# Scores and gate logits of an attention-plus-experts kernel, cut into more and smaller matmul tiles

## The chip, the cores and the metric

The kernel runs on one core of a Trainium2 chip (trn2). The metric is the device time of one execution in microseconds (us), the median of several runs; lower is better. TensorE is called PE here; a matmul on it consists of a load of the stationary operand (in the profile "PEld", LDWEIGHTS) and the streaming of the moving operand (MATMUL).

## What is computed

Chunked attention on four batches and eight heads (768 positions, head size 64), then a layer of eight experts with a fixed capacity. In numpy, cut to what matters:

```python
for c in range(S // 32):                      # chunks of 32 queries
    k_full = concat([mem_k, k[l_start:r_end]])     # 8 memory keys, 16 left, 32, 8 right
    a = softmax(q_c @ k_full.T / 8)
    out[c] = a @ v_full
x = out as (B*S, H*D) = (3072, 512)
logits = x @ w_gate                           # 8 experts
expert_idx, gate_w = argmax, its softmax probability
for e in range(8):                            # at most 80 tokens each, those of largest gate_w
    h = relu(x[tok_idx] @ w1[e]);  out[tok_idx] = gate_w * (h @ w2[e])
```

## The kernel before, in words

**Units and rounds.** Attention is cut into 32 units: a pair of heads (one on partitions 0 to 63, the other on 64 to 127), half of the sequence (384 queries in four groups of 96). Four units, the four head pairs of one batch and one half, make a round of 384 tokens; there are eight rounds.

**One unit.** Keys and queries are turned on PE (`turn_k` L325, `turn_q` L304) into `kT` and `qT`. `scores` (L773) makes, for each of the two heads, a tile `sp` of 128 keys by 384 queries. First one bf16 matmul a head adds the window mask for all queries (L779); then, for each of the four groups, one fp32 matmul a head (L786) has the group's 128 keys as stationary operand and its 96 queries as moving operand. As the heads lie on different partition halves, the two matmuls use different row halves of the array. ACT takes the exponential (L794). `values` (L351, matmul L357) multiplies with the values, 24 fp32 matmuls with 32 queries as stationary operand, into four column quarters of 32. DVE divides (L362), `turn_x` (L371) turns the output to `xT`, 128 channels by 384 tokens, which ACT copies to SBUF (L377).

**The gate of a round.** When the four `xT` of a round exist, `Ranks.steps` (L610) gives a list of small steps, two of which are popped in each later unit, between the other work. The first (`weigh`, L415) runs `gate_parts` (L384): four fp32 matmuls with a part of `w_gate` (padded from 8 to 32 columns, `wgc`) as stationary operand and 384 tokens as moving operand, one in each column quarter, which leaves four partial sums on four partition groups; ACT copies them (`lus`). The second (`logits`, L419) sums and turns them: three fp32 matmuls with 128 tokens of `lus` as stationary operand and a 0/1 matrix `sel4` as moving operand (L422). The later steps rank the tokens of each expert (L467 to L608).

**The last round** has no units behind it. Its logits are summed early (`early`, L806, matmul L810): for each of the four channel parts and three token groups one fp32 matmul with 128 tokens of `xT` as stationary operand and 8 columns of `wgc` as moving operand.

**Order.** The order of instructions on each engine is the order of the trace of the loop L852 to L905, fixed by `in_order`. The DMA queue SP loads keys and queries two head pairs ahead, values six units ahead, and in each unit two more pieces of 256 KB: expert weights or zeros for the output. After attention, 16 weight matrices of 2 MB (five of them already there) feed the experts (L1029 to L1063), at most about seven pieces in flight (`paced`, L162). The experts' matmuls (L1043, L1057) have 64 columns of weights as stationary operand and 80 tokens as moving operand.

Of the kernel before, what the change touches and what calls it, by code (L numbers as in the profile page):

```python
# [24 lines left out]
NG = 4  # L25
HT = NG * GQ
# [36 lines left out]
def kernel(  # L63
# [22 lines left out]
    NT = HT // 128  # L86
    NR = 2 * B
# [16 lines left out]
    const = ctx.enter_context(tc.tile_pool(name="const", bufs=1))  # L104
# [8 lines left out]
    mkey = masks[:, : 2 * WK].rearrange("p (f k) -> p f k", f=2)  # L113
    mqry = masks[:, 2 * WK : 2 * WK + 2 * HT].rearrange("p (f q) -> p f q", f=2)
    tok = masks[:, 2 * WK + 2 * HT :].rearrange("p (i m) -> p i m", i=2)
    wgc = const.tile([128, HP, 32], F32, name="wgc")
    sel4 = const.tile([128, E], F32, name="sel4")
    identb = const.tile([128, 128], BF16, name="identb")
    selq = const.tile([128, E], BF16, name="selq")

# [259 lines left out]
        def store(self, r, xr):  # L380
            nc.sync.dma_start(xd[r * HT : r * HT + HT, :].rearrange("(t p) d -> p t d", p=128), xr)


    def gate_parts(xTs, lu):  # L384

        for c in range(HP):
            nc.tensor.matmul(
                lu[32 * c : 32 * c + 32, :HT], lhsT=wgc[:, c, :], rhs=xTs[c], start=True, stop=True
            )

    full = [128, NT, E]

    class Ranks:
# [3 lines left out]
        def __init__(self, gt, ps_t):  # L397
            self.gt, self.ps_t = gt, ps_t
            tiles = dict(
                lus=([128, HT], F32), lmax=([128, NT], F32), lg=(full, F32), first=(full, F32),  # L400
                best=([128, NT], F32), el=(full, F32), oh=([128, NT, 4, E], BF16), gw=([128, NT], F32),
                ohg=(full, F32), rest=(full, F32), desc=([128, NT, ND, E], BF16), gbs=([128, HT], F32),
                ohT=([3 * E, HT], BF16), less=([128, NT, HT], BF16), older_=([128, NT, cap], BF16),
                beaten=([128, NT], F32), slo=([cap, E], BF16), hoto=([cap, E, cap], BF16),
                mores=([32 * NT, HT], BF16), own=(full, F32), ahead=([128, NT], F32), slot=([128, NT], BF16),
                hot=([128, NT, cap], BF16), left=([cap, E], BF16), stays=([cap, ND, E], F32),
                enters=([128, NT], F32), held=([cap, ND * E], F32), tab=([cap, ND, E], BF16), tabT=([3 * E, cap], BF16),
            )
            for name, (shape, kind) in tiles.items():
                setattr(self, name, gt.tile(shape, kind, name=name))  # L410
# [1 line left out]
        def ps(self, name, kind=F32):  # L412
            return self.ps_t.tile([128, 512 if kind == F32 else 1024], kind, name=name, tag="t")

        def weigh(self, xTs, lu):  # L415
            gate_parts(xTs, lu)
            nc.scalar.copy(self.lus, lu[:, :HT])

        def logits(self):  # L419
            lp = self.ps("lp")  # L420
            for t in range(NT):
                nc.tensor.matmul(  # L422
                    lp[:, E * t : E * t + E], lhsT=self.lus[:, 128 * t : 128 * t + 128], rhs=sel4,
                    start=True, stop=True,
                )
            self.largest(lp)

        def largest(self, lp):
# [178 lines left out]
            )  # L607
            nc.scalar.copy(self.tabT, tp[: 3 * E, :cap])  # L608

        def steps(self, r, xTs, lu):  # L610

            def fifth():
                self.turn_oh()
                self.count(0)
                self.count(1)

            def sixth():
                if r:
                    self.rivals()
                    self.beat()  # L620
                self.count(2)

            def seventh():
                if r:
                    self.older()
                self.sum_counts()

            return [
                lambda: self.weigh(xTs, lu), lambda: (self.logits(), self.gates()), lambda: None,
                lambda: (self.spread(), self.parts(r)), fifth, sixth, seventh,  # L630
                lambda: self.slots(r, self.turn_counts()), lambda: self.fill_old(r),
                lambda: self.hold(self.fill_new(r)), self.turn_table,
            ]
# [77 lines left out]
    with ExitStack() as actx:  # L711
# [16 lines left out]
        at.load_mv(0)  # L728
        at.load_v(0, 0)
        make_identity(nc, ident)  # L730
        nc.gpsimd.memset(wgc, 0.0)
        nc.scalar.dma_start(wgc[:, :, :E], moe_w_gate.rearrange("(c p) e -> p c e", p=128))

        def for_gates():
            prefi = gt.tile([128, E], I32, name="prefi")
            nc.gpsimd.iota(prefi, pattern=[[-1, E]], base=E, channel_multiplier=0)
            nc.gpsimd.tensor_copy(pref, prefi)
            by_q = ident.rearrange("p (q r e) -> p r e q", q=4, e=E)[:, 0]
            nc.vector.tensor_reduce(sel4, by_q, axis=AX, op=Alu.add)
            with nc.allow_low_precision("ones and zeros"):  # L740
                nc.vector.tensor_reduce(selq, by_q, axis=AX, op=Alu.add)
            nc.gpsimd.tensor_copy(identb, ident)
# [28 lines left out]
        P, o, xr, xTs, lus = {}, {}, {}, {}, {}  # L771

        def scores(i):  # L773
            n, f = units[i]
            sp = [ps_s.tile([WK, NG, GQ], F32, name="sp", tag="s") for e in range(2)]

            for e in range(2):
                r = slice(64 * e, 64 * e + 64)
                nc.tensor.matmul(  # L779
                    sp[e].rearrange("p g q -> p (g q)"), lhsT=mkey[r, f, :], rhs=mqry[r, f, :],  # L780
                    start=True, stop=False,
                )
            for g in range(NG):
                for e in range(2):
                    r = slice(64 * e, 64 * e + 64)
                    nc.tensor.matmul(  # L786
                        sp[e][:, g], lhsT=at.kT[n][r, NG * f + g, :],
                        rhs=at.qT[n][r, HT * f + GQ * g : HT * f + GQ * g + GQ], start=False,
                        stop=g == NG - 1,
                    )  # L790
            P[i] = []
            for e in range(2):
                P[i].append(wk.tile([WK, NG, GQ], F32, name="P", tag="P"))
                nc.scalar.activation(P[i][e], sp[e], Act.Exp, scale=scale)  # L794
# [11 lines left out]
        def early(cs, lp):  # L806

            for c in cs:
                for t in range(NT):
                    nc.tensor.matmul(  # L810
                        lp[:, E * t : E * t + E], lhsT=xTs[HP * (NR - 1) + c][:, 128 * t : 128 * t + 128],
                        rhs=wgc[:, c, :E], start=False, stop=c == HP - 1 and t == NT - 1,
                    )


        turns = {0: [("k", 2), ("q", 2)], 1: [("k", 3), ("q", 3)]}
        for n in range(HP, NP):
            i = 2 * n - 6
# [4 lines left out]
        ranks = Ranks(gt, ps_x)  # L823
        start = len(list(nc.cur_bb.bb.instructions))
# [27 lines left out]
        for i in range(NU):  # L852
            n, f = units[i]
            r = i // HP
            if i + 1 < NU:
                scores(i + 1)
# [14 lines left out]
                at.turn_q(i + 2)  # L871
            values(i)
            if i and i % HP == 0:
                lus[r] = ps_x.tile([128, 512], F32, name="lu", tag="t")
                steps = ranks.steps(r - 1, [xTs[i - HP + c] for c in range(HP)], lus[r])
# [37 lines left out]
        r = NR - 1  # L913
# [234 lines left out]
    with tc.If(redo[1] > 0):  # L1148

        with ExitStack() as actx:  # L1150
# [5 lines left out]
            ps_l = actx.enter_context(tc.tile_pool(name="ps_l2", bufs=1, space=PSUM))  # L1156
            at = Attention(actx, ps_t, wpool.tile([128, 4, F], F32, name="ld2", tag=f"w{WR0}", bufs=1))
# [5 lines left out]
            ranks = Ranks(gt, ps_t)  # L1163
            for i, (n, f) in enumerate((HP * b + c, f) for b in range(B) for f in range(2) for c in range(HP)):
                r, c = i // HP, i % HP
# [42 lines left out]
                xTs.append(at.turn_x(i, xr, ps_t.tile([128, 512], F32, name="xt2", tag="t")))  # L1208
                if c == HP - 1:
                    at.store(r, xr)  # L1210
                    steps = ranks.steps(r, xTs, ps_l.tile([128, 512], F32, name="lu2", tag="l"))
# [48 lines left out]
```

## Time and profile before

| | |
|---|---|
| time, three runs | 250.19, 251.43, 253.89 us; median 251.43 |
| span of the profiled run | 246.5 us, 11417 instruction records |
| attention with the ranks of the rounds | to about 140 us |
| last ranks, gathering of the first expert | to about 151 us |
| experts | 151 to 240 us |
| L786 scores | 512 records of MATMUL, 64x128 stationary, 96 moving, mean 269 ns; their loads 189 ns |
| L779 masks | 64, mean 333 ns |
| L387 and L422, gate | 56 of 495 ns and 42 of 254 ns |
| L810, early logits | 24 of 254 ns |

How to read it: a line of the groups gives line, engine, operation, output<-input, stationary shape (rows*columns), moving shape, count, then total busy time and mean of one. Matmuls overlap, so their busy times may sum to more than the time that passes; the pace of a group is read from starts in the timeline. "idle before <- releaser" is how long the engine stood still ahead of a group and what ended that; "issue" means that nothing the profile shows ended it. An fp32 matmul that is no transpose shows as two passes, each with its load. The rows of tenths are 40 equal slices of the span.

### The profile page before, as it was taken

Reading aid. Unit: us, or ns where it says so; the run is one execution under the profiler, and the core shown is the slowest. Engines: PE = TensorE matmul, PEld = TensorE weight load, DVE = VectorE, ACT = ScalarE, POOL = GpSimd, SP = SyncE. Lnnn points to the kernel's source line nnn. Section 1 sums busy time; section 2 is a strip of 40 time slices with the busy share of each in tenths; the row PEclk is TensorE's granted clock in tenths of the full one; section 3 lists DMA queues with packets and bytes.
Section 4 is the critical chain, followed back from the end, with each engine's and each line's share of the span. In section 5 each row is a group of like instructions: output and inputs, shape, how many; then the busy total and the mean of one; then the engine's idle time right before and its main releaser. Section 6 shows DMA issues by size and latency. Waiting matters only on the chain. (4 is left out here: it accounts for less than half of the span.)

```text
span 246.5 us, 11417 instructions
## 1 busy us (share of the span) xinstructions
PE 228.3 (93%) x4976; PEld 200.6 (81%) x4976; DVE 105.5 (43%) x288; ACT 81.8 (33%) x198; POOL 80.5 (33%) x182
## 2 busy tenths in 40 slices
PE   5979999999999999999899999969799997999980
PEld 3857889798888788888778889959799996999970
DVE  3333447758579477585555862000112111110240
ACT  2245555665555573665545301100000101010000
POOL 2454947537275182450412147300101010110111
PEclk9999999999999999999999889989999999999996
DMA  6999999999999999999999899999999998890101
GB/s 205 284 283 298 279 296 325 340 370 321 341 364 330 376 331 334 370 278 329 302 305 372 264 363 307 295 333 298 311 335 313 358 288 284 277 332 28 32 29 37
DMA packets 69879, 70.97 MB, mean 288 GB/s; under 512 B 38204, under 2 KB 46396, under 8 KB 69820
## 3 DMA queue, kind: packets, MB, share of 16 engines
q1 hardware_dynamic: 67836, 67.17, 87.4%
q0 software_dynamic: 1024, 2.62, 3.5%
q8 instruction: 41, 0.67, 1.2%
q10 hardware_dynamic: 960, 0.36, 0.6%
q14 instruction: 18, 0.15, 0.2%
HBM read 56.24 MB, written 13.89 MB: 285 GB/s over the span
## 5 line engine op out<-in xcount | busy, mean ns | idle before, releaser
L794 ACT ACTIVATE P<-sp 128x384 f32<-128x384 f32 x64 | 27.9, 488 | 29.6 <-PE sp L786 29.6
L1043 PE MATMUL hp<-xn,w 128*64 128x80 f32 x896 | 33.7, 233 | 3.0 <-issue 3.0
L1043 PEld LDWEIGHTS hp<-xn,w 128*64 128x64 f32 x896 | 32.1, 137 | 3.9 <-issue 3.4
L786 PEld LDWEIGHTS sp<-qT,kT 64*128 64x128 f32 x512 | 33.2, 189 | 1.5 <-issue 0.9
L786 PE MATMUL sp<-qT,kT 64*128 64x96 f32 x512 | 33.5, 269 | 0.9 <-ACT qT L316 0.4
L1057 PE MATMUL yt<-hT,w 128*64 128x80 f32 x896 | 34.2, 239 | 0.0
L1057 PEld LDWEIGHTS yt<-hT,w 128*64 128x64 f32 x896 | 33.0, 142 | 1.2 <-issue 1.1
L1047 ACT ACTIVATE hT<-hp 128x320 f32<-128x320 f32 x16 | 7.0, 437 | 70.7 <-PE hp L1043 70.7
L1111 POOL DMA_INDIRECT out_dram<-y,idx_s x7 | 6.4, 917 | 73.0 <-DVE y L1110 73.0
L357 PE MATMUL o<-vw,P 128*32 128x65 f32 x1536 | 28.9, 222 | 0.7 <-issue 0.7
L357 PEld LDWEIGHTS o<-vw,P 128*32 128x32 f32 x1536 | 23.5, 109 | 6.3 <-issue 5.4
L346 DVE COPY kT<-pt 128x480 f32<-128x480 f32 x32 | 19.9, 666 | 16.3 <-PE pt L343 8.2
L268 POOL COPY vw<-mv 8x512 f32<-8x512 f32 x32 | 22.4, 703 | 8.7 <-DMA vw<-in_v_dram 8.7
L1022 DVE COPY xn<-xp 128x320 f32<-128x320 f32 x7 | 3.4, 491 | 39.4 <-PE xp L1020 39.4
L366 DVE TENSOR_TENSOR xr<-o,over_s 128x384 f32<-128x384 f32 x32 | 17.8, 558 | 1.1
L316 ACT COPY qT<-pt 128x384 f32<-128x384 f32 x31 | 16.0, 582 | 4.8 <-PE pt L315 4.8
L377 ACT COPY xT<-xt 128x384 f32<-128x384 f32 x32 | 15.7, 489 | 4.7 <-PE xt L375 4.7
L330 POOL COPY kh<-ld 128x768 f32<-128x768 f32 x15 | 12.3, 822 | 13.7 <-PE more L549 8.3
L375 PE MATMUL xt<-ident,xr 128*128 128x128 f32 x96 | 16.5, 281 | 0.0
L315 PE MATMUL pt<-ident,qh 128*128 128x128 f32 x96 | 15.0, 291 | 1.2 <-DVE kT L346 1.2
L1063 DVE COPY ys<-yt 128x320 f32<-128x320 f32 x7 | 3.4, 492 | 28.7 <-PE yt L1057 28.7
L531 DVE SCALAR_TENSOR_TENSOR less<-gbs,gw,behind 128x384 bf16<-128x384 f32 x21 | 15.0, 745 | 0.0
(162 smaller groups left out, 305.2 us busy)
## 6 DMA issues: line engine op xcount, KB each, us to landing
w<-in_moe_w_dram SPq DMA_DIRECT2D x120, 256.0 KB, 5.2
vw<-in_v_dram SPq DMA_DIRECT2D x60, 128.0 KB, 5.3
ld<-in_k_dram SPq DMA_DIRECT2D x16, 384.0 KB, 5.6
ld<-in_q_dram SPq DMA_DIRECT2D x16, 384.0 KB, 6.4
xd<-xr SPq DMA_DIRECT2D x8, 768.0 KB, 5.8
out_dram<-zero SPq DMA_DIRECT2D x24, 256.0 KB, 4.9
ld<-in_moe_w_dram SPq DMA_DIRECT2D x8, 256.0 KB, 6.0
vw<-in_v_dram SPq DMA_DIRECT2D x4, 96.0 KB, 5.6
```

Of the source, the lines that this page charges most:

```text
L268: nc.gpsimd.tensor_copy(self.vw[n, f][:MS, :, :, :D], self.mv[b][:, h : h + 2].unsqueeze(2).to_broadcast([MS, 2, NG, D]),)
L315: nc.tensor.transpose(pt[:, t, :], qh[:, t0 + t].rearrange("p e d -> p (e d)"), ident)
L316: out[t0 // 3](qT.rearrange("p (x t) -> p x t", t=T0)[:, :, t0 : t0 + 3], pt.rearrange("p t x -> p x t"))
L346: nc.vector.tensor_copy(win[:, :, :, u0 : u0 + 3], _ap(pt, 0, [pt.ap[0], [JG, G], [1, (WK - MS) // T0], [step, 3]]),)
L357: nc.tensor.matmul(out[32 * i : 32 * i + 32, e, t, :], lhsT=P[e][:, g, CHUNK * c : CHUNK * c + CHUNK], rhs=self.vw[n, f][:, e, g, :], star ...
L366: nc.vector.tensor_tensor(out=xr[:, :, 128 * c : 128 * c + 128].rearrange("p t (e d) -> p e t d", e=2), in0=o[:, :, :, :D], in1=over_s[:, ...
L375: nc.tensor.transpose(xt[:, 128 * t : 128 * t + 128], xr[:, t, 128 * c : 128 * c + 128], ident)
L377: nc.scalar.copy(xT, xt[:, :HT])
L786: nc.tensor.matmul(sp[e][:, g], lhsT=at.kT[n][r, NG * f + g, :], rhs=at.qT[n][r, HT * f + GQ * g : HT * f + GQ * g + GQ], start=False, sto ...
L794: nc.scalar.activation(P[i][e], sp[e], Act.Exp, scale=scale)
L1043: nc.tensor.matmul(hp[j : j + 64, f, :], lhsT=w1[:, c, f1 : f1 + 64], rhs=xns[e][:, c, :], start=c == 0, stop=c == DK - 1,)
L1057: nc.tensor.matmul(yt[j : j + 64, d, :], lhsT=w2[:, f, d * 128 + j : d * 128 + j + 64], rhs=hTs[e][:, f, :], start=f == 0, stop=f == FK - 1,)
```

## The change

Each head's scores are made in two halves of 64 keys, so that a group is four matmuls with 64x64 stationary operands, two row halves times two column halves of the array, in place of two with 64x128; the masks likewise. The gate's logits are made in one step, straight from `xT`: for each token group of 128, each channel part and each quarter of 32 tokens one fp32 matmul, the 32 tokens being the stationary operand (one column quarter of the array) and the 8 columns of `w_gate` the moving one; the four channel parts accumulate. This takes away `gate_parts`, `lus` with its copy on ACT, and `sel4`, and `wgc` shrinks to its 8 columns. `early` is cut into quarters in the same way. The purpose is to use the parts of the array side by side and to load fewer columns of weights for few moving columns.

```diff
-    wgc = const.tile([128, HP, 32], F32, name="wgc")
-    sel4 = const.tile([128, E], F32, name="sel4")
+    wgc = const.tile([128, HP, E], F32, name="wgc")
...
-        for c in range(HP):
-            nc.tensor.matmul(
-                lu[32 * c : 32 * c + 32, :HT], lhsT=wgc[:, c, :], rhs=xTs[c], start=True, stop=True
-            )
...
-        def weigh(self, xTs, lu):
-            gate_parts(xTs, lu)
-            nc.scalar.copy(self.lus, lu[:, :HT])
-
-        def logits(self):
-            lp = self.ps("lp")
+        def logits(self, xTs, lp):
+
             for t in range(NT):
-                nc.tensor.matmul(
-                    lp[:, E * t : E * t + E], lhsT=self.lus[:, 128 * t : 128 * t + 128], rhs=sel4,
-                    start=True, stop=True,
-                )
+                for c in range(HP):
+                    for j in range(0, 128, 32):
+                        nc.tensor.matmul(
+                            lp[j : j + 32, E * t : E * t + E], lhsT=xTs[c][:, 128 * t + j : 128 * t + j + 32],
+                            rhs=wgc[:, c, :], start=c == 0, stop=c == HP - 1,
+                        )
             self.largest(lp)
...
-                lambda: self.weigh(xTs, lu), lambda: (self.logits(), self.gates()), lambda: None,
+                lambda: self.logits(xTs, lp), self.gates, lambda: None,
...
-            for e in range(2):
-                r = slice(64 * e, 64 * e + 64)
+            quarters = [(e, slice(64 * e, 64 * e + 64), slice(h, h + 64)) for e in range(2) for h in (0, 64)]
+            for e, r, h in quarters:
                 nc.tensor.matmul(
-                    sp[e].rearrange("p g q -> p (g q)"), lhsT=mkey[r, f, :], rhs=mqry[r, f, :],
+                    sp[e][h].rearrange("p g q -> p (g q)"), lhsT=mkey[r, f, h], rhs=mqry[r, f, :],
                     start=True, stop=False,
                 )
             for g in range(NG):
-                for e in range(2):
-                    r = slice(64 * e, 64 * e + 64)
+                for e, r, h in quarters:
                     nc.tensor.matmul(
-                        sp[e][:, g], lhsT=at.kT[n][r, NG * f + g, :],
+                        sp[e][h, g], lhsT=at.kT[n][r, NG * f + g, h],
                         rhs=at.qT[n][r, HT * f + GQ * g : HT * f + GQ * g + GQ], start=False,
                         stop=g == NG - 1,
                     )
...
-                    nc.tensor.matmul(
-                        lp[:, E * t : E * t + E], lhsT=xTs[HP * (NR - 1) + c][:, 128 * t : 128 * t + 128],
-                        rhs=wgc[:, c, :E], start=False, stop=c == HP - 1 and t == NT - 1,
-                    )
+                    for j in range(0, 128, 32):
+                        nc.tensor.matmul(
+                            lp[j : j + 32, E * t : E * t + E],
+                            lhsT=xTs[HP * (NR - 1) + c][:, 128 * t + j : 128 * t + j + 32], rhs=wgc[:, c, :],
+                            start=False, stop=c == HP - 1 and t == NT - 1,
+                        )
```

More of the change, by code (lines that the diff above doesn't have):

```diff
@@ L381, in store @@
             nc.sync.dma_start(xd[r * HT : r * HT + HT, :].rearrange("(t p) d -> p t d", p=128), xr)
-    def gate_parts(xTs, lu):
-        for c in range(HP):
-            nc.tensor.matmul(
-                lu[32 * c : 32 * c + 32, :HT], lhsT=wgc[:, c, :], rhs=xTs[c], start=True, stop=True
-            )
     full = [128, NT, E]
@@ L399, in __init__ @@
             tiles = dict(
-                lus=([128, HT], F32), lmax=([128, NT], F32), lg=(full, F32), first=(full, F32),
+                lmax=([128, NT], F32), lg=(full, F32), first=(full, F32),
                 best=([128, NT], F32), el=(full, F32), oh=([128, NT, 4, E], BF16), gw=([128, NT], F32),
@@ L608, in turn_table, with steps @@
             nc.scalar.copy(self.tabT, tp[: 3 * E, :cap])
-        def steps(self, r, xTs, lu):
+        def steps(self, r, xTs, lp):
             def fifth():
@@ L730 @@
         make_identity(nc, ident)
-        nc.gpsimd.memset(wgc, 0.0)
-        nc.scalar.dma_start(wgc[:, :, :E], moe_w_gate.rearrange("(c p) e -> p c e", p=128))
+        nc.scalar.dma_start(wgc, moe_w_gate.rearrange("(c p) e -> p c e", p=128))
         def for_gates():
@@ L738, in for_gates @@
             by_q = ident.rearrange("p (q r e) -> p r e q", q=4, e=E)[:, 0]
-            nc.vector.tensor_reduce(sel4, by_q, axis=AX, op=Alu.add)
             with nc.allow_low_precision("ones and zeros"):
@@ L770 @@
         units = [(HP * b + c, f) for b in range(B) for f in range(2) for c in range(HP)]
-        P, o, xr, xTs, lus = {}, {}, {}, {}, {}
+        P, o, xr, xTs = {}, {}, {}, {}
         def scores(i):
@@ L873 @@
             if i and i % HP == 0:
-                lus[r] = ps_x.tile([128, 512], F32, name="lu", tag="t")
-                steps = ranks.steps(r - 1, [xTs[i - HP + c] for c in range(HP)], lus[r])
+                lr = ps_x.tile([128, 512], F32, name="lr", tag="t")
+                steps = ranks.steps(r - 1, [xTs[i - HP + c] for c in range(HP)], lr)
                 later = deque(
@@ L1210 @@
                     at.store(r, xr)
-                    steps = ranks.steps(r, xTs, ps_l.tile([128, 512], F32, name="lu2", tag="l"))
+                    steps = ranks.steps(r, xTs, ps_l.tile([128, 512], F32, name="lr2", tag="l"))
                     for step in steps[: None if r < NR - 1 else 4]:
```

## The prediction

> **What bounds the kernel now.** I read the busy table and the 40 slices first, then the busy time by stage, then the matmul groups, then the DMA queues, and last the timeline at the places where TensorE stops.
>
> ```profile
> PE 228.3 (93%) x4976; PEld 200.6 (81%) x4976; DVE 105.5 (43%) x288; ACT 81.8 (33%) x198; POOL 80.5 (33%) x182
> PE   5979999999999999999899999969799997999980
> ```
>
> TensorE has work in nearly every slice. All that the change touches lies in the first 140 us (attention with the rounds of the gate beside it), so the stages matter:
>
> ```profile
> 20.00:60.00 40.00, 39.62 (x887) 33.54 (x885) 23.91 (x62) 23.59 (x56) 23.61 (x57) 1.00 1.10 322
> 60.00:100.00 40.00, 39.76 (x827) 33.24 (x825) 27.47 (x75) 22.10 (x55) 17.89 (x38) 1.00 1.11 344
> 100.00:140.00 40.00, 39.27 (x900) 33.10 (x898) 26.43 (x81) 21.23 (x56) 12.02 (x33) 1.00 0.98 321
> ```
>
> Columns: stage, its length, busy us (and number) of PE, PEld, DVE, ACT, POOL, clock, DMA share, GB/s. PE has no gap to speak of, at full clock; the other engines have room. The DMA engines are as full as PE (share about 1, 320 to 345 GB/s). A shorter PE chain would thus shorten this stage, unless something feeding PE has no room left. Something has none: its own instructions.
>
> ```profile
> q1 hardware_dynamic: 46492, 39.09, 105.0%
> q8 instruction: 21, 0.34, 1.2%
> ```
>
> These are the queues from 20 to 140 us: packets, MB, share. Queue 8 carried 21 packets of 16 KB. In the same stage PE and PEld have 2608 and 2606 records; with a few semaphore records, 256 to a packet. Over the whole run it is 41 packets for 9952. So one packet is 256 records of PE; an fp32 matmul costs four (two passes, each a weight load and a matmul), a bf16 matmul or a transpose two.
>
> ```profile
> 121.56 0.53 PE L357 MATMUL o<-vw,P 128*32 128x65 f32 x18
> 122.82 0.65 PE L357 MATMUL o<-vw,P 128*32 128x65 f32 x30 [0.73 <-issue]
> ```
> ```profile
> 157.77 2.79 PE L1043 MATMUL hp<-xn,ld 128*64 128x80 f32 x73
> 162.84 0.35 PE L1043 MATMUL hp<-xn,ld 128*64 128x80 f32 x2 [2.28 <-issue]
> ```
>
> Here PE stops in the middle of a group, waiting for nothing the profile names ("issue"). Counting records in order, five stops (81.1, 121.9, 160.3, 173.8, 204.6 us) all fall at the same place, 0.75 of a block of 256 counted from the first record; in each a packet of queue 8 landed 1.2 to 1.5 us (mean 1.4) before PE went on. Outside the stops, a packet never starts before PE has passed such a place; late in the run, with the other queues empty, it starts 0.04 to 0.2 us after it and lands by 1.3 us. With the queues full it lands 2.2 to 5.3 us after (mean of the 22 in attention 3.5). So the next block is asked for when PE enters a block, and PE has that one block's time in hand. A fetch cycle is 3.5 + 1.4 = 4.9 us in the full stage; PE now takes about 5.8 us over a block there. The margin is small and was overrun twice before 140 us (0.4 and 0.9 us).
>
> [...] loads of 32, 64 and 128 columns show 109, 137 and 189 ns, 0.83 a column. [...] 0.2 us from the last scores matmul to the transposes behind it, and quarters overlapping at L357.
>
> **The change, part by part: work on PE.** Matmul records of 65 and 384 columns last 222 and 486 ns: 0.83 ns a column and pass.
> *Scores.* Before, two row halves go side by side; on each a pass follows the last after 111 ns (128 columns of weights at 0.83 are 107), 84 ns the first time. Eight passes: 84 + 6 x 111 = 0.75 us start to start. After, four tiles of 64x64, each pass 96 x 0.83 + 2 = 82 to 84 ns of streaming with 53 ns of loading beside it, as L1043 shows (80 columns, 64 of weights, one pass after 69 ns): 7 x 84 = 0.59. Saved 0.16 us a unit, 32 units: 5.3 us. If the tiles did not overlap in both directions it would be 0.75 lost a unit; L786 overlaps rows, L357 columns, and I take the saving. Masks: four loads of 64 columns for two, side by side; nothing[...].
> *Gate of a round.* Removed: L387, 0.78 us (63.99 to 64.77), and L422, 6 x 0.11 = 0.67. Added: 96 passes of 32 columns of weights and 8 moving, in 24 groups of four. A group takes at least its load, 27 + 4 = 31 ns (0.75 us), at most the 56 ns of L357 (1.34). I take 0.8 and save 0.65; seven rounds: 4.6 us.
> *Early logits* (L810): 24 passes of 0.11 = 2.7 us become 96 in 0.8: 1.9 us saved.
> The copy of lus (ACT, 0.48 us a round), the memset of wgc and sel4 go: nothing, ACT and POOL have room, and the steps behind the gate have slack of several units. Together PE's own work shrinks by 11.8 us.
>
> **The change: instructions.** Scores 256 matmuls to 512: +1024 records. Masks 64 to 128: +128. Gates 98 to 672: +1148. Early 12 to 48: +144. Together +2444, or 9.5 blocks, all before 140 us, where PE now runs through 21.9. A round of four units (16.0 us now, for instance 67.85 to 84.15 and 84.15 to 100.18 between values) holds 4 x 150 + 28 + about 72 = 700 records, 2.7 blocks; after, 4 x 186 + 192 + 72 = 1008, 3.9 blocks. PE would like to do them in 16.0 - 4 x 0.16 - 0.65 = 14.7 us. But they are uneven: the block with the gate is 192 records in 0.8 us and 64 more in 1 us, so 1.8 us, and the other 2.9 share 12.9 us, 4.4 each. Each block takes the longer of its work and the fetch cycle. The cycle is 4.9 us in full traffic; in the emptier first 40 us packets landed after 3.15 on average, 4.6 with the 1.4; and a slower attention spreads the same 40 MB thinner still. Estimate: 4.3. The gate's block takes 4.3; the others, where 4.4 of work meets 4.3 of fetch with a scatter of some 0.8 on either side, about 4.7: 4.3 + 2.94 x 4.7 = 18.1 us, 2.1 more than now. Seven rounds: +14.7. The first round without a gate (186 records in 2.9 us, so 256 in 4.1) breaks even; the early logits save 1.9 and cost 0.56 of a block, 2.4, with the gaps around them about +1.5 in all. Sum: +16; 251.4 + 16.5 = 268.
>
> Nothing hides these waits: PE is in order, and ACT, DVE, POOL and the loads, whose buffers PE frees, wait behind it. The experts (same instructions, weights requested from the same point on) shift as they are.
>
> **Rivals.**
> *A. Fetches keep up, PE's work decides.* For it: PE is full to 99% and at the end a fetch landed in 1.3 us, cycle 2.7. Against: that is with empty queues. Gives 251.4 - 11.8 = 239.6; DMA could take back a few us, as 40 MB in 12 us less asks for 360 GB/s. This is the faster side.
> *B. The thinner traffic shortens the cycle to 3.6 us.* A round: 3.6 + 2.94 x 4.45 = 16.7, +0.7; seven and the rest: +5, 256. For it: waiting in queue 8 is 2.4 of the 3.5 us. Against: the early stage at 290 GB/s gave 3.15.
> *C. The cycle stays at 4.9, or the stops also cost clock.* 4.9 + 2.94 x 5.1 = 19.9, +3.9 a round, +27: 279. In favour: after the 2.3 us stop the clock was halved for 3.4 us (slices at 0.8). Against: the shorter stops show none.
>
> **How the numbers follow.** Forecast 0.63, A 0.12, B 0.15, C 0.10. The time is 268. For the range, low 252 leaves out A and a little of B; high 283 takes in C and the scatter of stops in the experts (5 us of them in this profile). Slower than 256.4: all of the forecast and C and near a third of B, 0.77. Within 2%: most of B, 0.12. Faster than 246.4: A, less if DMA holds it: 0.11.
>
> **What would show it.** In the changed profile: about 50 packets on queue 8 and 6200 matmul records; idle time of PE put down to "issue" in most rounds, next to the gate's matmuls, 25 to 30 us in all before the experts; scores of 32 records in about 0.8 us with their drain, the gate's 96 in about 0.8 us; attention ending near 156 us for 140; experts as long as before. Wrong if PE stays full in attention with 50 packets (A), or if scores take longer than now per unit between stops (tiles don't overlap), or if the stops don't fall on blocks of 256.

## The result and the profile after

The changed kernel takes 280.38 us (median; 279.30 to 282.68), the kernel before beside it 250.81. The ratio is 1.118, with a 95% interval of 1.109 to 1.128: slower, by 29.6 us. The forecast was 268, with a range of 252 to 283. Some executions of a kernel take a few per cent longer than the others; ratios here use the quicker ones alone, and where too few of these were measured there is no ratio.

The head of the page of the changed kernel (span, busy times, two rows of the 40 slices):

```profile
span 277.5 us, 13850 instructions
...
PE 233.0 (84%) x6198; PEld 204.5 (74%) x6198; DVE 104.4 (38%) x287; ACT 79.4 (29%) x191; POOL 79.3 (29%) x181
...
PE   5987858969959959949969599968999999989980
...
PEclk9999968968968959959979979979999999999996
```

PE was busy in nearly every slice before. Now a dip comes about every three slices (7 us each) up to slice 23 and then stops: one dip for each round of attention. The row of the clock dips with or just after each of them. The dip in slice 27 is the step from attention to the experts; behind it both rows are near 9, as before.

The stages of the changed kernel (stage, its length, busy us and number of PE, PEld, DVE, ACT, POOL, clock, DMA share, GB/s):

```profile
20.00:60.00 40.00, 30.92 (x958) 26.26 (x954) 16.81 (x45) 15.86 (x36) 17.42 (x42) 0.88 0.92 275
60.00:100.00 40.00, 33.45 (x962) 28.16 (x955) 21.43 (x56) 17.86 (x44) 15.55 (x34) 0.84 0.91 278
100.00:140.00 40.00, 34.00 (x1014) 28.91 (x1014) 22.85 (x64) 17.87 (x44) 14.74 (x33) 0.85 0.89 274
...
183.30:270.70 87.40, 83.63 (x2109) 79.44 (x2109) 13.73 (x28) 7.01 (x16) 9.98 (x11) 0.98 0.78 251
```

In each 40 us PE now stands still for 6 to 9 us, where it stood still for 0.2 to 0.7, and the clock is 0.84 to 0.88 where it was 1.00. No other engine took up the time: DVE, ACT and POOL are less busy than before, and so are the queues (0.9 for 1.0 to 1.1). The last row is the experts: 87.1 us from their first to their last matmul, 88.8 before. The first of them starts at 183.3 for 150.9, so the whole loss lies ahead of that.

The instruction queue and the groups that the change made (group: busy us, mean ns, idle time before it and what ended that):

```profile
q8 instruction: 50, 0.82, 1.2%
...
L773 PE MATMUL sp<-qT,kT 64*64 64x96 f32 x1024 | 32.0, 265 | 8.0 <-issue 7.3
```

50 packets for 41, with 12,396 records of PE for 9,952: again one packet for about 256. The list of waits puts the idle time to "issue", and to the new matmuls (us in all, times, longest):

```profile
PEld lr L411 <- issue: 12.8, 4, 3.5
PE lr L411 <- issue: 12.5, 4, 3.4
...
PE sp L773 <- issue: 7.3, 3, 3.5
```

One gate in the timeline (start, us, line, tiles, count of passes; a name in brackets is idle time):

```profile
53.70 0.89 PE L356 MATMUL o<-vw,P 128*32 128x65 f32 x48
54.41 0.82 PE L411 MATMUL lr<-wgc,xT 128*32 128x8 f32 x72
57.98 0.51 PE L411 MATMUL lr<-wgc,xT 128*32 128x8 f32 x24 [2.76 <-issue]
58.42 0.53 PE L767 MATMUL sp<-masks 64*64 64x384 bf16 x4
58.74 1.49 PE L773 MATMUL sp<-qT,kT 64*64 64x96 f32 x32
60.16 1.54 PE L314 MATMUL pt<-ident,qh 128*128 128x128 f32 x6
...
64.34 0.83 PE L773 MATMUL sp<-qT,kT 64*64 64x96 f32 x32
65.09 0.87 PE L342 MATMUL pt<-ident,kh 128*128 128x128 f32 x6
```

PE stops inside the gate after 72 of its 96 passes, at the border of a block of records. When it goes on, everything runs at half speed: the same 32 passes of the scores take 1.42 us start to start at 58.74 and 0.75 at 64.34. The record of the clock has 6.8 us at half from 57.5.

Between 20 us and the last mask matmul of attention (130.8 us before, 162.9 after, so 32.0 later) the trace of the changed kernel has 11 stops, steps of over 0.45 us from the start of one matmul to the start of the next, 28.7 us together; before it had 3 with 2.0. Ten of the 11 lie at the border of a block. The clock is halved for 40.5 us, before not at all; 7.8 us of that fall into stops, so half of the other 32.7, 16.4 us, are lost work. The array's saving, from starts in the timelines, is 32 x (0.95 - 0.76) for the scores and 7 x (1.45 - 0.97) for the gates, 9.4 us. 26.7 + 16.4 - 9.4 = 33.7, against 32.0; each stop counted from start to start takes in one ordinary step, 0.2 us or so, which makes the sum a little too long.

### The profile page after: what moved, and what is told of

Its sections match the earlier page's. It is cut to its first block, busy times and chain, and to the rows that moved or that the text cites. A ratio compares the mean times of both kernels' runs of the same rounds, so it can differ in the third digit from the quotient of the medians.

```text
span 277.5 us, 13850 instructions
## 1 busy us (share of the span) xinstructions
PE 233.0 (84%) x6198; PEld 204.5 (74%) x6198; DVE 104.4 (38%) x287; ACT 79.4 (29%) x191; POOL 79.3 (29%) x181
## 5 line engine op out<-in xcount | busy, mean ns | idle before, releaser
L1032 PE MATMUL hp<-xn,w 128*64 128x80 f32 x896 | 35.7, 238 | 5.3 <-issue 5.0
L773 PE MATMUL sp<-qT,kT 64*64 64x96 f32 x1024 | 32.0, 265 | 8.0 <-issue 7.3
L773 PEld LDWEIGHTS sp<-qT,kT 64*64 64x64 f32 x1024 | 29.4, 150 | 10.2 <-issue 8.1
L356 PE MATMUL o<-vw,P 128*32 128x65 f32 x1536 | 32.4, 236 | 2.0 <-issue 1.9
L356 PEld LDWEIGHTS o<-vw,P 128*32 128x32 f32 x1536 | 26.4, 119 | 9.0 <-issue 8.9
L345 DVE COPY kT<-pt 128x480 f32<-128x480 f32 x32 | 19.9, 667 | 15.9 <-ACT P L781 7.9
L444 POOL TENSOR_TENSOR desc<-oh,masks 128x24 bf16<-128x24 bf16 x16 | 3.3, 228 | 69.4 <-DVE oh L436 69.4
L374 PE MATMUL xt<-ident,xr 128*128 128x128 f32 x96 | 19.0, 313 | 0.2 <-DVE xr L365 0.2
L314 PE MATMUL pt<-ident,qh 128*128 128x128 f32 x96 | 18.0, 332 | 1.2 <-DVE kT L345 1.2
L411 PE MATMUL lr<-wgc,xT 128*32 128x8 f32 x672 | 8.3, 182 | 12.5 <-issue 12.5
L315 ACT COPY qT<-pt 128x384 f32<-128x384 f32 x31 | 16.6, 573 | 5.1 <-PE pt L314 4.7
L411 PEld LDWEIGHTS lr<-wgc,xT 128*32 128x32 f32 x672 | 7.4, 115 | 12.9 <-issue 12.8
```

The lines of the kernel that those rows point to most:

```text
L314: nc.tensor.transpose(pt[:, t, :], qh[:, t0 + t].rearrange("p e d -> p (e d)"), ident)
L315: out[t0 // 3](qT.rearrange("p (x t) -> p x t", t=T0)[:, :, t0 : t0 + 3], pt.rearrange("p t x -> p x t"))
L345: nc.vector.tensor_copy(win[:, :, :, u0 : u0 + 3], _ap(pt, 0, [pt.ap[0], [JG, G], [1, (WK - MS) // T0], [step, 3]]),)
L356: nc.tensor.matmul(out[32 * i : 32 * i + 32, e, t, :], lhsT=P[e][:, g, CHUNK * c : CHUNK * c + CHUNK], rhs=self.vw[n, f][:, e, g, :], star ...
L374: nc.tensor.transpose(xt[:, 128 * t : 128 * t + 128], xr[:, t, 128 * c : 128 * c + 128], ident)
L411: nc.tensor.matmul(lp[j : j + 32, E * t : E * t + E], lhsT=xTs[c][:, 128 * t + j : 128 * t + j + 32], rhs=wgc[:, c, :], start=c == 0, stop ...
```

## The experiments

**How a round depends on its records.** All runs are gathered here, for the text below. A round is the mean over the six rounds from unit 4 to unit 27 (counted from 0), from mask matmul to mask matmul, in the one execution that was profiled; the records of PE in it, with its few semaphore records, are counted, and divided by 256 give blocks. "Stops" and "half clock" are us per round. The column "5.0 x blocks" is what fetching alone takes at 5.0 us a block (how that is measured stands under "The fetch cycle" below). Times are medians of all executions, and ratios are against the kernel before on the same chip.

| kernel | records | blocks | 5.0 x blocks | round, us | stops | half clock | time, us | ratio, 95% interval |
|---|---|---|---|---|---|---|---|---|
| before | 685 | 2.68 | 13.4 | 15.4 | 0.1 | 0 | 247 to 251 | 1 |
| scores in halves, values merged | 701 | 2.74 | 13.7 | 15.6 | 0.4 | 0 | 246.09 | 0.990, 0.984 to 0.996 |
| values merged alone | 557 | 2.18 | 10.9 | 15.9 | 0 | 0 | 248.79 | none |
| gate halves, values merged | 624 | 2.44 | 12.2 | 16.0 | 0 | 0 | 248.71 | 1.004, 0.999 to 1.009 |
| gate halves alone | 752 | 2.94 | 14.7 | 15.8 | 0.4 | 0 | 249.26 | 1.020, 1.005 to 1.034 |
| scores, gate halves, values merged | 768 | 3.00 | 15.0 | 16.5 | 1.2 | 0 | 249.95 | 1.005, 0.999 to 1.010 |
| scores alone | 829 | 3.24 | 16.2 | 17.5 | 2.0 | 2.3 | 260.35 | 1.064, 1.051 to 1.076 |
| gate quarters alone | 848 | 3.31 | 16.6 | 18.1 | 2.2 | 2.3 | 266.44 | 1.088, 1.061 to 1.116 |
| changed, values merged | 864 | 3.38 | 16.9 | 18.9 | 2.8 | 2.8 | 268.58 | 1.076, 1.067 to 1.086 |
| changed, gate in halves | 897 | 3.50 | 17.5 | 18.2 | 2.7 | 1.7 | 266.56 | 1.089, 1.072 to 1.106 |
| changed, gate spread | 990 | 3.87 | 19.3 | 20.0 | 4.1 | 4.0 | 277.12 | none |
| changed | 992 | 3.88 | 19.4 | 20.2 | 3.8 | 6.3 | 280.38 | 1.118, 1.109 to 1.128 |

**1. The scores alone.** The kernel before, with masks and scores in halves as in the change, gate and early logits as before:

```diff
+            quarters = [(e, slice(64 * e, 64 * e + 64), slice(h, h + 64)) for e in range(2) for h in (0, 64)]
...
-                        sp[e][:, g], lhsT=at.kT[n][r, NG * f + g, :],
+                        sp[e][h, g], lhsT=at.kT[n][r, NG * f + g, h],
```

> The kernel before with only the scores and masks in column halves; gate and early logits as before. Fetch theory (PE waits for its own instruction blocks of 256 records; a long stop then halves its clock): 844 records a round, 3.3 blocks, about 4.6 us of work each against a fetch cycle of about 4.5: few stops, under 1.5 us each, no halved clock window of 6.8 us; 45 packets on the instruction queue; a round of four units about 15.7 us for 16.0 before, time 247 to 253. Tile theory (the smaller tiles themselves or the changes between tile shapes cost the time): the scores are the larger part of the new matmuls, so most of the 30 us shows here, over 260. If only PE's own work counts: 245.

Measured 260.35, ratio 1.064. By its time alone the rival, that the small tiles cost time themselves, would have it. The trace says otherwise. The scores' own pace is the changed kernel's, and the idle time lies before the values' matmuls, which this kernel did not touch:

```profile
PEld o L357 <- issue: 15.9, 38, 2.8
...
PE o L357 <- issue: 9.3, 9, 2.7
```

The same two rows of the kernel before:

```profile
PEld o L357 <- issue: 5.4, 28, 0.9
...
PE o L357 <- issue: 0.7, 1, 0.7
```

The stops within the six rounds all fall on borders of blocks. The fetch theory was right in kind and missed in size: the expectation took a cycle of 4.5 us, and the trace has 5.0. It also expected no long half of the clock, and 13.7 us of it came before the end of attention, 6.8 of them in one stretch.

**2. The gate alone.** The changed kernel with the scores of before:

```diff
-            for e, r, h in quarters:
+            for e in range(2):
+                r = slice(64 * e, 64 * e + 64)
...
-                        sp[e][h, g], lhsT=at.kT[n][r, NG * f + g, h],
+                        sp[e][:, g], lhsT=at.kT[n][r, NG * f + g, :],
```

> The changed kernel with the scores and masks of before; the gate's and the early logits' matmuls in quarters. Fetch theory: 864 records a round, 3.4 blocks, 192 of them in 0.8 us. The block with the gate is the only short one, and where its border falls moves by 0.4 of a block from round to round, so some rounds stop for about 3 us inside or just behind the gate and run half the clock after it, others stop for less than 1.5 us and keep the clock: 262 to 275, and all stops at the same place of a block of 256. Tile theory: same length of every gate in every round, and no stop. Data-wait theory (the gate's matmuls wait for a copy or a buffer that the profile does not name): a stop of about 3 us at the same matmul in each of the seven rounds, 275 to 282.

Measured 266.44, as the fetch theory had it. It also speaks against a wait of the gate for its data: the long stops of the rounds fall in turn into L356, L374, L411, L356, L774, L411, L356 (values, turned output, gate, values, scores, gate, values), always at the border of a block and not at one instruction. A first gate of this kernel in the timeline:

```profile
31.95 0.89 PE L356 MATMUL o<-vw,P 128*32 128x65 f32 x48
32.66 1.04 PE L411 MATMUL lr<-wgc,xT 128*32 128x8 f32 x96
33.63 0.34 PE L767 MATMUL sp<-masks 64*128 64x384 bf16 x2
...
35.90 0.65 PE L356 MATMUL o<-vw,P 128*32 128x65 f32 x29
37.94 0.26 PE L356 MATMUL o<-vw,P 128*32 128x65 f32 x4 [1.40 <-issue]
```

Here no border lies inside the gate. Its 96 passes run through in 0.97 us, start to next start, and the bill comes in the values one unit later.

**3. The burst or the count.** The changed kernel with the gate's matmuls spread: 12 of them in each of three later units, the last 12 in the gate's step, the 12 of a unit going into free columns of the PSUM tile of the values, all added up by DVE. The number of PE records is that of the changed kernel:

```diff
+        def share(self, xT, c, lp):
+            for t in range(NT):
+                for j in range(0, 128, 32):
+                    nc.tensor.matmul(
+                        lp[j : j + 32, E * t : E * t + E], lhsT=xT[:, 128 * t + j : 128 * t + j + 32],
+                        rhs=wgc[:, c, :], start=True, stop=True, skip_group_check=True,
+                    )
...
+            if given:
+                ranks.share(xTs[i - 2], (i - 2) % HP, part)
```

> The changed kernel, with the gate's matmuls taken apart: the 12 of each of the first three units of a round are issued two units later, ahead of that unit's values, into free columns of its PSUM tile, and VectorE adds the parts up in SBUF; only the last 12 stay in the gate's step. Same number of matmuls, no burst of 192 records. Fetch theory: still 3.9 blocks a round, now about 3.7 us of work each against a cycle of about 4.4: many stops of up to 1.5 us, no long one, so no or few halved clock windows; a round 17 to 18 us, time 256 to 266. If the clock alone were the loss: below 250. Data-wait and tile theories: the work is the same and the loss stays, 275 or more.

Measured 277.12: the expectation fell, and by the number alone it is the rivals' side (275 or more) that came true. The trace is against them: the stops within the rounds all lie on borders of blocks, and experiments 2 and 5 speak against a wait for data and against the tiles. Without the burst there are more stops, most of them shorter, but together they take about the same (4.1 us a round for 3.8), the clock is still halved for 4.0 us a round, and a round is 20.0 us for 20.2. So at this count the number of blocks goes with the length of a round, and spreading the gate did not help.

**4. Fewer records for the same gate.** The changed kernel with gate and early logits in column halves of 64 tokens, half as many matmuls:

```diff
-                    for j in range(0, 128, 32):
+                    for j in range(0, 128, 64):
...
-                            lp[j : j + 32, E * t : E * t + E], lhsT=xTs[c][:, 128 * t + j : 128 * t + j + 32],
+                            lp[j : j + 64, E * t : E * t + E], lhsT=xTs[c][:, 128 * t + j : 128 * t + j + 64],
```

> The changed kernel with gate and early logits in two halves of 64 tokens in place of four quarters of 32: half as many matmuls there, of about the same time on the array (12 groups of two at about 57 ns, 0.7 us a gate). Scores in column halves stay. Fetch theory: 912 records a round, 3.6 blocks; the block with the gate is 96 records in 0.7 us and 160 in 3 us, so it stops for about 1 us and not 3, and the clock holds: a round 15.5 to 16.5, time 246 to 257. Tile theory and data-wait theory: no great difference to the changed kernel, 272 to 282.

Measured 266.56, 14 us less than the changed kernel, and 2.0 us less a round, though the array is slower at it: a gate in halves takes 1.50 us, start to next start, in quarters 0.97.

```profile
64.33 1.57 PE L411 MATMUL lr<-wgc,xT 128*64 128x8 f32 x48
65.83 0.34 PE L767 MATMUL sp<-masks 64*128 64x384 bf16 x2
```

(This timeline is of the kernel of experiment 6, with the same gate and no stop in it.) The direction was right; 246 to 257 was too low: as in experiment 1 the cycle was taken too short, and the clock did not hold (1.7 us at half a round).

**5. The same scores with fewer records elsewhere.** Experiment 1, with the values' matmuls merged wherever two neighbouring chunks of 32 queries belong to one group: 8 for 12 a head.

```diff
-            for t in range(NT):
+            pairs = [(0, 0, 2), (1, 2, 2), (1, 0, 2), (2, 2, 2)]
+            singles = [(2, 0, 1), (2, 1, 1), (0, 2, 1), (0, 3, 1)]
+            for part in (pairs, singles):
...
-                            out[32 * i : 32 * i + 32, e, t, :], lhsT=P[e][:, g, CHUNK * c : CHUNK * c + CHUNK],
+                            out[32 * i : 32 * (i + w), e, t, :],
+                            lhsT=P[e][:, g, CHUNK * c : CHUNK * (c + w)],
```

> The scores in column halves as in the run with the scores alone (260.4), and the values' matmuls merged where two neighbouring chunks of 32 queries belong to one group: 8 matmuls a head for 12, four of them with 64 queries as stationary operand. A unit then has 186 - 32 = 154 PE records, against 150 before and 186 with the scores alone; the whole run about 10,080 against 9952 and 11,104, some 41 to 42 packets of instructions. If the number of records times the fetch cycle sets the time, the loss goes away: 242 to 253, stops in attention under 4 us together (14 with the scores alone). If instead the 64x64 tiles or the masks in halves cost the time themselves, it stays at 257 or above, since the values were not slow: the same scores are in it.

Measured 246.09, ratio 0.990: the loss of experiment 1 is gone with the 32 records a unit, the scores being the same. This is the run that decides between fetches and tiles. Four rows of its timeline:

```profile
105.91 0.36 PE L782 MATMUL sp<-masks 64*64 64x384 bf16 x4
106.09 0.83 PE L788 MATMUL sp<-qT,kT 64*64 64x96 f32 x32
106.85 0.88 PE L315 MATMUL pt<-ident,qh 128*128 128x128 f32 x6
...
108.35 1.05 PE L359 MATMUL o<-vw,P 128*64 128x65 f32 x32
109.33 0.28 PE L513 MATMUL over<-oh,older__171 128*80 128x8 bf16 x3
```

The scores take 0.76 us; in the kernel before, from 104.75 to 105.71, 0.96:

```profile
104.75 1.03 PE L786 MATMUL sp<-qT,kT 64*128 64x96 f32 x16
105.71 0.88 PE L315 MATMUL pt<-ident,qh 128*128 128x128 f32 x6
...
107.21 0.89 PE L357 MATMUL o<-vw,P 128*32 128x65 f32 x48
108.03 0.28 PE L510 MATMUL over<-oh,older__171 128*80 128x8 bf16 x3
```

The merged values, though, take 0.98 for 0.82, so a unit gains next to nothing (rounds of 15.6 and 15.4). The 1% isn't seen in attention: its last mask is at 131.0 for 130.8. In the profiles the experts take 85.0 for 88.8, with the same instructions and shorter stops among them. Whether that is where the 1% comes from wasn't tried.

**6. The gate in halves alone**, on the kernel before with the early logits in halves too; scores and values as before:

```diff
-        def weigh(self, xTs, lu):
-            gate_parts(xTs, lu)
-            nc.scalar.copy(self.lus, lu[:, :HT])
...
+                    for j in range(0, 128, 64):
+                        nc.tensor.matmul(
+                            lp[j : j + 64, E * t : E * t + E], lhsT=xTs[c][:, 128 * t + j : 128 * t + j + 64],
+                            rhs=wgc[:, c, :], start=c == 0, stop=c == HP - 1,
+                        )
```

> Scores as before; the gate straight from the turned output, but in column halves of 64 tokens: 24 matmuls a round, 96 PE records, against 28 before, 192 to 288 with quarters. A round has 768 records, three blocks of 256, for 700 before. By count of records times a fetch cycle of 5.0 us: 3.0 x 5.0 = 15.0 us at least, against 16.0 that PE needs for the work, so only blocks that are worked off faster than the cycle stop: 248 to 257, stops in attention under 8 us. If the gate's direct form costs by itself (waits on the turned output, accumulation in one tile), it comes out near the 266 of the run with quarters.

Measured 249.26, ratio 1.020 (1.005 to 1.034): the direct gate costs far less when its records are few (2.0% for the 8.8% of experiment 2), though the interval still lies above 1. The array's time for it is as before (1.50 us for 0.78 + 0.67), and stops take 0.4 us a round.

**7 and 8. Emptier queues.** The changed kernel and the kernel before, both with the expert weights and the zeros of the output held back until attention is over. All are still loaded and stored, so the experts wait for them and the whole times (319.37 and 291.47) say nothing of the question.

```diff
-            for _ in range(2 if i >= 4 else 0):
-                bulk = slow if slow and (i >= NU - 6 or i % 4 < 3) else nothing
...
-        assert not slow
-        for dma in nothing:
+        for dma in [*slow, *nothing]:
```

> The changed kernel, with the loads of expert weights and the zeros for the output held back until the end of attention; all are still done. In attention the queues then carry about 24 MB in place of 41. Read from the end of attention (first matmul of the experts may wait for weights, so the last mask matmul counts) and from the time that a packet of instructions takes after the request. If the traffic of the queues makes the fetch long: the packet lands after 1.5 to 2.5 us in place of 3.4, the stops fall under 10 us together (28 in the changed kernel), no clock is halved after them, and the last mask is at 130 to 142 us for 162.9. If the fetch takes its 5 us whatever the queues carry: the last mask stays at 158 us or later. The whole time is of no use for this, since the weights come late.

> The kernel before with the same loads held back, as the yardstick of the run above. Its packets have room already, so fetch theory: last mask 126 to 131 us (130.8 before). If the changed kernel with the same hold-back ends its attention level with this one or up to 8 us earlier (its work on PE is 11.8 us less by the forecast's account), the array work of the change is a gain that only the fetches hide; if it ends more than 5 us later, there is a cost beside the fetches.

Stages of the changed kernel with its loads held back:

```profile
60.00:100.00 40.00, 33.58 (x998) 28.43 (x994) 22.08 (x60) 17.83 (x44) 15.45 (x34) 0.84 0.63 174
100.00:140.00 40.00, 35.40 (x1022) 30.07 (x1014) 22.04 (x61) 17.88 (x45) 14.69 (x33) 0.84 0.44 119
```

The queues are at 0.63 and 0.44 for 0.9, and PE is hardly fuller. Its last mask is at 157.7 us for 162.9; the kernel before with the same hold-back has it at 128.6 for 130.8. The first side of the expectation fell. The second has its time (158 us or later) within 0.3 us, but not its reason: the traffic does matter, though little. A packet landed 2.8 us after the request on average for 3.3. Parted by what the queues did in the 2.5 us after the request: 2.0 us (12 packets) with the queues under 0.3 busy, 3.4 (12 packets) with them over 0.9. After a stop, with idle queues, it is still 2.1 to 2.4 us, and PE goes on 1.5 us after the landing: a cycle of 3.7 us at best, while the block with the gate is worked off in about 2 (0.97 for the gate's 192 records, about 1 for the other 64, estimated as in the forecast). So each gate still stops PE for 2 to 4 us and the clock is still halved after it. By the yardstick of the second expectation, 29 us between the two kernels would mean a cost beside the fetches; but with 24.7 us of stops and 36 us of half clock the fetches were not out of the way, and the yardstick doesn't apply. Whether the change would pay without them isn't settled by this pair.

**9. The merged values alone**, on the kernel before (the diff of experiment 5, without the scores).

> The kernel before with the merged values alone (118 PE records a unit for 150, 572 a round): tells whether the 1% of the run with scores in halves and merged values (0.990 of before) comes from the scores or from the records saved. The array's own time for the values doesn't change (the quarters are as long busy as they were). If the scores brought it: 0.995 to 1.005 of before, 246 to 250. If sparing the last stops of the kernel before brought it (1.9 us in attention): 0.985 to 0.995, and the scores in halves are worth nothing.

Measured 248.79, beside 248.09 of the kernel before, with no ratio. No stop is left in the rounds, and a round is 15.9 us for 15.4: the values do not take the same time on the array, as the expectation had it, but 0.16 us more a unit, as experiment 5 showed. So the records spared are worth little to the kernel before, and merging costs about what halving the scores brings.

**10. The changed kernel with merged values** (the diff of experiment 5 on the changed kernel).

> The changed kernel with the values merged and nothing else: 880 records a round for 1008, 3.44 blocks for 3.94, the burst of the gate as it was. By records: 3.44 x 5.0 = 17.2 us a round, and 0.9 above it as in the other runs, so 18.1, and 262 to 270. If the gate's burst of 192 records and the half clock after it are the main loss and the number of records is not, it stays above 274.

Measured 268.58, ratio 1.076, within the expectation: 128 records a round less, the gate's burst unchanged, and 12 us back (1.2 us a round), although the array has 5 us more to do (32 x 0.16).

**11 and 12. All of it lean.** The kernel of experiment 6 with the merged values of experiment 5, and the same with the scores in halves.

> Scores as before, gate and early logits in halves of 64 tokens, values merged: 640 records a round, 2.5 blocks, 12.5 us by fetches, far below the 15.5 us that PE needs for the work. No stop should be left in attention, and the gain of the direct gate shows by itself: 0.98 to 0.995 of before, 242 to 248. If the direct gate is worth nothing on the array, it comes out at the time of the merged values alone.

> All of the change's ideas with fewer records: scores in column halves, values merged, gate and early logits in halves of 64 tokens: 784 records a round, 3.06 blocks, 15.3 us by fetches against about 14.9 of PE's work. Fetch theory: at the edge, 0.985 to 1.02 of before, a few stops at the gate. If it comes out above 1.03, the count alone does not price the change; if below 0.98, the array gain of the forecast is real and nearly whole.

Measured 248.71 (1.004) and 249.95 (1.005): neither beats the kernel before. The first has no stop in the rounds and misses 242 to 248 by little: it comes out at the time of the merged values alone (248.79), since the direct gate in halves gains nothing on the array. The second is within its own, at the edge as expected: 3.0 blocks a round and 1.2 us of stops, which eat the scores' gain.

## Why the prediction was right, and where it was short

**What bounds, and the kind of loss: right.** PE's order of work bounds attention (PE busy for 39.3 to 39.8 of each 40 us before), and in these traces its instructions came in blocks of about 256 records (12,396 in 50 packets). The count was exact: +2,444 records, 50 packets, 6,198 matmuls. The ten long stops of attention lie where stops were said to be, all at 0.75 of a block counted from the first record, and in each a packet landed 1.3 to 1.6 us before PE went on. Experiments 5, 4 and 10 show the cause: fewer records for the values took the whole loss of the scores away (5) and 12 us of the change's 30 (10), fewer records for the gate 14 us (4), though none of the three made the array's own work shorter than in the kernel that it started from.

**The array's own time: right within 0.5 us in sum, with misses of opposite sign in the parts.** Scores were to save 0.16 us a unit and saved 0.19 to 0.20. The four tiles do overlap in both directions: in the changed kernel four passes, of about 240 ns each, start within 10 to 20 ns, and the next four 82 ns after the first. The 0.17 us from the start of the last scores matmul to the transposes behind it (0.20 before) is in that figure. The gate was put at 0.8 us and took 0.97, so it saved 0.48 and not 0.65 a round. The early logits run 48 passes in 0.52 us, where 0.4 was taken:

```profile
165.89 0.59 PE L798 MATMUL pt<-wgc,xT 128*32 128x8 f32 x48
166.41 0.28 PE L483 MATMUL mp<-tabT,ohT 24*128 24x80 bf16 x3
```

6.2 + 3.4 + 1.7 = 11.3, for 11.8.

**The fetch cycle: mis-sized.** The step that failed is "Estimate: 4.3". Taken from requests to landings in attention, the packets of the changed kernel landed after 3.34 us (28 packets), those of before after 3.48, and PE went on 1.5 us after the landing (mean of the ten stops): 4.8 us, not 4.3. In the five rows of the table from "scores alone" to "changed, gate spread" the same sum is 4.7 to 5.1; the table uses 5.0. The reason given, that a slower attention spreads the traffic thinner, was tested in experiment 7: thinning it far more, to half, brought 0.5 us. With 5.0 in the forecast's own working, 5.0 + 2.94 x 5.1 gives 20.0 us a round; 20.2 was measured. A second term was off: the forecast took a round of before as 16.0 us, from two rounds, where the six average 15.4, so its 18.1 was 2.7 us more a round and not 2.1.

**The clock: left to a rival.** "The shorter stops show none" was right of nearly all stops of 1.5 us and less (2 of 40, below), but the forecast did not ask how long its own stops would be. In the rounds they come to 2.9 to 4.6 us, and those cost clock: 40.5 us at half, 16.4 us of work. The stops alone came to 28.7 us, where the forecast had 25 to 30. So by the account of stops and clock the 12 us that it lacks, 268 for 280, are the clock, and by the account of blocks and cycles they are the cycle (and the 16.0). The two terms don't look independent. A block worked off at half clock takes longer (the scores of a unit 1.42 us for 0.75, above), which leaves the next one more time to land: the changed kernel and experiment 3 have 6.3 and 4.0 us of half clock a round and the same 20 us. Experiment 4 has 32 records a round more than experiment 10, and yet its round is shorter, 18.2 us for 18.9, with 1.7 us of half clock for 2.8. So there the clock does seem to cost, though these two differ in the gate's burst as well. How much the clock would cost on its own can't be told from these runs; none of them could hold it up.

**The rivals.** Rival C, a cycle that stays at 4.9 or stops that cost clock, gave 279 and is what happened, by both of its halves; it had 0.10 and should have had more than B, whose thinner traffic was an argument and C's halved clock a reading. That the measured time lies in the forecast's range is owed to the room left for C, not to the working of the forecast itself. A and B are out: PE was not full, and the cycle did not shrink. That the experts would be as long as before was right (87.1 us for 88.8); attention was to end near 156 us and ended near 163.

Crossing from block to block cost the kernel before next to nothing: with 685 records in 15.4 us it takes 5.75 us over a block, above the cycle of 5.0, and has 0.1 us of stops a round. The changed kernel, whose work is about 3.7 us a block (estimate: 15.4 - 4 x 0.19 - 0.48 us in 3.88 blocks), has 3.8 us of stops a round.

## What to carry to other kernels

Count the instruction records of an engine before cutting its work finer: blocks of 256 times the fetch cycle of the trace (here 5.0 us beside full queues) was a floor under a round in every kernel of the table: they lie 0.6 to 5 us over it, furthest where the work itself is far above the floor. Matmuls that were faster on the array could cost more here than they saved, by taking more instructions (an fp32 one four records): the scores in halves saved 0.19 us a unit and, alone, made a round of four units 2.1 us longer (17.5 for 15.4). And where a stop is forecast, work out its length: of the 28 stops in attention over 2.2 us, 26 were followed by a halved clock (below).

## What the runs showed of the hardware that was not expected

- The fetch of PE's instructions was slow even beside nearly idle queues: in experiment 7 a packet took 2.0 us to land with the queues under 0.3 busy, for 3.4 with them over 0.9, and after a stop PE went on 1.5 us later still. In these runs emptier queues were thus a weak remedy (experiment 7: 5 us of attention), fewer records a strong one (experiments 4, 5 and 10: 12 to 14 us).
- After long stops the clock was halved, mostly for 3.4 or 6.8 us. Over all the profiles here, 26 of the 28 stops in attention that lasted over 2.2 us had a half clock within 5 us of their start, 9 of the 23 between 1.5 and 2.2 us, and 2 of the 40 between 0.6 and 1.5 us (stops inside a half clock left out).
- Stationary operands of 64 columns in place of 32, under a moving operand of 65 or 8 columns, took longer in all although there were fewer matmuls: merged values 0.98 us for 0.82, a gate in halves 1.50 for 0.97.
